# Bias tests on three engines and both bias sums on VectorE; the halves of a head's output added by GpSimd

## The chip, the cores and the metric

The kernel runs on one core of one Trainium2 chip. The core has five engines that run beside each other and meet at semaphores: TensorE (PE in the profile: matmuls, with PEld for its weight loads), VectorE (DVE), ScalarE (ACT), GpSimd (POOL) and SyncE (SP, which here only issues DMAs). The metric is the device time of one execution in microseconds, median of the runs. Each engine works through its own instructions in the order in which they stand in the program; an instruction that waits holds up all that stand behind it on that engine.

## The reference, cut to what matters

```python
scale = 1 / sqrt(64);  B, H, S, D = 2, 8, 576, 64;  hidden = 32
x = log1p(|i - j|) / log1p(max(i, 1))                      # i, j = 0..575
bias[h, i, j] = sum_d w2[d, h] * relu(x * w1[d] + b1[d])   # one for both batches
attn = softmax(scale * q @ k.T + bias)                     # float32
y = attn @ v                                               # (2, 8, 576, 64)
# then two feed-forward stages of matmuls over the 1152 rows of y ("moe" and "moe2")
```

The change lies in the first two stages alone: the bias, and the attention.

## The kernel before

**Order.** Nothing is moved by a scheduler: the instructions stand on each engine as the Python loops write them. Buffers come from pools of a fixed number of tiles, and whoever writes a tile again waits until its last readers are done.

**Bias.** relu(x*w1+b1) of a hidden unit changes slope at a knot, so the bias is a sum over tests "is |i-j| above the threshold of row i". One test tile `s` (128 partitions = 4 rows i by 32 hidden units, 576 columns j) is written per group g by `gen_s(g)`; there are 144 (`NG4`). `on_act` sends 3 of 8 to ScalarE as a steep sigmoid with bias `nthr` (L305), the others to VectorE as a comparison with `thr` (L307). `bias_mm(g16)` (L333) multiplies four test tiles by small weights `wb` into two PSUM tiles, `ps[0]` and `ps[1]`; there are 36 such steps (`NG16`). `bias_ev` (L343, L345) takes ScalarE to scale `ps[0]` into `t` and GpSimd to multiply `t` by a table `l16` (VectorE for the last two, `LASTV`); `bias_out` (L350) lets VectorE scale `ps[1]`, add `t` and write `bo`, which goes to DRAM. In step g16 the tests of step g16+2 are written. `sp` holds 12 test tiles. Ahead of the loop VectorE works out the knots (`one`, `eu`, `thr`, `nthr`; L236 to L265) and the weights (`big`, `sc`, `ab`, `wf`, `wb`; L269 to L296), one after the other, and the first eight tests stand among them. `prep_head(0, ...)`, GpSimd's high and low parts of q, k and v of head 0, is strewn over the odd steps.

**Attention.** 72 units u, nine per head (k = u mod 9), in a software pipeline with a step s per unit. In step s: TensorE's scores of unit s (`u_qk`, tile `sc`), its transposes of unit s-3 (`pt`, `pl`); VectorE's sum of scores and bias with row maximum of unit s-1 (`u_max`, tile `ng`, L430); ScalarE's exponential of unit s-2 (`u_exp`, L441) and high part of the transposed unit s-4 (`pth`, L505); VectorE's low part (`ptl`, L506). A head's product with v, `pv`, is made a head later in three chunks and ended at `EV`: k = 3 (512 columns), 6 and 8 (320 each). `pv` has its even part in one half of the partitions, its odd part in the other; `pv_ev` lets ScalarE copy one half across to `pvt` (L554) and VectorE add the other from PSUM (L556) into `x32`. `pvt` has two buffers. GpSimd makes the parts of the next head (`prep_head`, L66 and L195; v at k = 6 and 8) and, every second head, `x_out` (L568 to L570): six instructions in steps with k = 2 and 4 that multiply `x32` by 1/sum (`r`, brought by DMA) and split it for the next stage. `r` has one buffer, and SP brings it through DRAM (`r_d`), in line with the bias loads.

Of the kernel before, what the change touches and what calls it, by code (L numbers as in the profile page):

```python
# [55 lines left out]
def make_body(stop=None):  # L56
    def body(tc, a):
# [21 lines left out]
        with ctx, tc.manual_schedule():  # L79
# [128 lines left out]
            with ExitStack() as bctx:  # L208
# [37 lines left out]
                ts(sg, w1r, 0.0, ALU.is_ge, 2.0, ALU.mult)  # L246
                ts(sg, sg, -1.0, ALU.add)
                ts(dn, w1r, sg, ALU.mult, 1e-30, ALU.max)
                V.reciprocal(out=dn, in_=dn)
                ts(kap, b1r, sg, ALU.mult, dn, ALU.mult)  # L250

                ts(v, c4, kap, ALU.mult, -8.0, ALU.max)
                ts(v, v, 8.0, ALU.min, -1.4426950408889634, ALU.mult)
                ts(kf, v, MAGIC, ALU.add)
                ts(kf, kf, -MAGIC, ALU.add)
                V.tensor_tensor(out=f, in0=v, in1=kf, op=ALU.subtract)
                ts(pw.bitcast(I32), kf, 127.0, ALU.add, 2.0 ** 23, ALU.mult)
                taylor = [np.log(2.0) ** n / math.factorial(n) for n in range(8)]
                ts(po, f, float(taylor[7]), ALU.mult)
                for n in range(6, 0, -1):  # L260
                    V.scalar_tensor_tensor(out=po, in0=po, scalar=float(taylor[n]), in1=f, op0=ALU.add, op1=ALU.mult)
                V.scalar_tensor_tensor(out=po, in0=po, scalar=1.0, in1=pw, op0=ALU.add, op1=ALU.mult)
                ts(thr, po, sg, ALU.mult, sg, ALU.subtract)
                ts(rs, rr, sg, ALU.mult)

# [3 lines left out]
                V.tensor_reduce(out=m2, in_=w2a.rearrange("p (d h) -> p d h", h=H), op=ALU.max, axis=AX.X,  # L269
                                apply_absolute_value=True)  # L270
                V.tensor_reduce(out=m1, in_=wb1.rearrange("p (d t) -> p d t", t=2), op=ALU.max, axis=AX.X,
                                apply_absolute_value=True)
                V.tensor_tensor(out=m1, in0=m1, in1=m2, op=ALU.mult)
                V.tensor_reduce(out=top, in_=m1, op=ALU.max, axis=AX.X)
                V.tensor_scalar(out=top, in0=top, scalar1=2.0 ** -90, scalar2=None, op0=ALU.max)
                V.tensor_scalar(out=sc.bitcast(I32)[:, 0:1], in0=top.bitcast(I32), scalar1=0x7F800000, scalar2=0x7F800000,
                                op0=ALU.bitwise_and, op1=ALU.bitwise_xor)
                V.tensor_scalar(out=sc.bitcast(I32)[:, 1:2], in0=top.bitcast(I32), scalar1=0x7F800000, scalar2=None,
                                op0=ALU.bitwise_and)
                V.tensor_scalar(out=sc[:, 0:1], in0=sc[:, 0:1], scalar1=512.0, scalar2=None, op0=ALU.mult)  # L280
# [821 lines left out]
```

## Time and profile before

| | us |
|---|---|
| median of 3 runs (1149.09 to 1151.95) | 1149.34 |
| the profiled execution | 1150.27 |
| its span | 1148.5 |
| PE busy over the span | 1115.9 (97%) |
| DVE, ACT, POOL busy over the span | 711.9, 506.7, 373.3 |
| bias, from the first test to the last sum | 13.4 to 83.0 |
| attention, to the last exponential | 83 to 214 |

The profiled execution lies 0.93 us above the median, and 1.8 us of it lie around the span. Over the whole span TensorE is the busy engine; in the first 214 us VectorE is, with ScalarE and GpSimd close by, and the change lies there. A row of the timeline has start, length, engine, line, operation, output and input, and the count of merged instructions; in square brackets the idle time ahead of it and what ended that.

### The profile page before, as it was taken

The page shows a single profiled execution, that of the slowest core. Times are in us where ns is not written, and L with a number is a line of the kernel's source. Part 1 is how long each engine was busy: PE and PEld are TensorE (multiplying, and loading weights), DVE is VectorE, ACT ScalarE, POOL GpSimd, SP SyncE. Part 2 cuts the span into 40 slices and gives each one's busy share as a digit, 9 for nine tenths or more (in the row PEclk, how much of TensorE's full clock was granted, in tenths as well). Part 3 has the DMA queues.
Part 4 walks back from the last instruction along what each step waited for, and adds up shares of the span by engine and source line. Part 5 has one row for each costly group of instructions (what it writes and reads, how often), then busy time and mean ns, then how long its engine had stood idle before and what let it go on. Part 6 is the DMA issues. An engine that isn't in the chain of part 4 may idle for free.

```text
span 1148.5 us, 18982 instructions
## 1 busy us (share of the span) xinstructions
PE 1115.9 (97%) x7578; PEld 999.8 (87%) x7578; DVE 711.9 (62%) x1241; ACT 506.7 (44%) x879; POOL 373.3 (33%) x307
## 2 busy tenths in 40 slices
PE   6989999999999999999999999999999999999998
PEld 3448889999999899898998989989899898998986
DVE  7999999787752766554645636446365463554633
ACT  5988988633333553341522505325143151341520
POOL 3996789222212613220311202113022131220310
PEclk8999999999999999999999999999999999999999
DMA  3666665123310210210201102112021120210102
GB/s 140 229 230 216 210 187 166 41 92 110 111 42 14 93 37 13 62 47 28 74 26 49 49 27 74 37 38 70 14 65 40 34 74 10 64 47 28 56 19 82
DMA packets 35286, 87.45 MB, mean 76 GB/s; under 512 B 5439, under 2 KB 5630, under 8 KB 34302
## 3 DMA queue, kind: packets, MB, share of 16 engines
q1 hardware_dynamic: 35054, 85.96, 23.5%
q8 instruction: 59, 0.97, 0.3%
q10 hardware_dynamic: 144, 0.29, 0.1%
q14 instruction: 29, 0.24, 0.1%
HBM read 73.23 MB, written 13.01 MB: 75 GB/s over the span
## 4 chain that ended last, share of the span: by engine, by line
PE 70%; DVE 16%; issue 4%; ACT 2%; DMA 1%; DVEq 0%; ACTq 0%; SPq 0%
PE d L1014 34%; PE x L932 11%; PE y L932 8%; PE z L932 8%; PE o L810 3%; DVE ng L430 3%; DVE ptl L506 3%; PE m L584 2%; DVE ww L105 1%; DVE ww L108 1%; DVE ww L110 1%; DVE pth L506 1%; DVE x L556 1%; DMA wf<-in_moe_w 1%; ACT ww L104 1%
## 5 line engine op out<-in xcount | busy, mean ns | idle before, releaser
L1025 DVE SCALAR_TENSOR_TENSOR acc<-d,P,acc 128x512 f32<-128x512 f32 x135 | 101.3, 750 | 240.1 <-PE d L1014 240.0
L1000 POOL TENSOR_TENSOR w2l<-w2r,w2h 128x512 fp32r<-128x512 f32 x64 | 94.0, 1470 | 465.3 <-ACT w2h L999 457.0
L1014 PE MATMUL d<-w2h,hh 128*128 128x512 f32 x576 | 225.0, 391 | 0.0
L1014 PE MATMUL d<-w2h,hl 128*128 128x512 f32 x576 | 224.7, 390 | 0.0
L1014 PE MATMUL d<-w2l,hh 128*128 128x512 f32 x576 | 224.3, 389 | 0.0
L940 ACT ACTIVATE s<-x 128x576 f32<-128x576 f32 x96 | 62.5, 651 | 355.3 <-PE x L932 352.1
L945 ACT ACTIVATE hh<-s 128x576 fp32r<-128x576 f32 x128 | 87.9, 687 | 95.6 <-DVE s L957 46.3
L1014 PEld LDWEIGHTS d<-w2h,hl 128*128 128x128 f32 x576 | 108.1, 188 | 23.1 <-DVE hl L950 0.3
L1014 PEld LDWEIGHTS d<-w2l,hh 128*128 128x128 f32 x576 | 108.2, 188 | 22.1
L1014 PEld LDWEIGHTS d<-w2h,hh 128*128 128x128 f32 x576 | 108.2, 188 | 21.8
L950 DVE SCALAR_TENSOR_TENSOR hl<-s,hh 128x576 fp32r<-128x576 f32 x128 | 103.4, 826 | 1.7 <-ACT hh L945 1.5
L750 POOL TENSOR_TENSOR w1l<-wf,w1h 128x768 fp32r<-128x768 f32 x32 | 59.3, 1853 | 76.6 <-ACT w1h L749 76.6
L932 PE MATMUL x<-xth,w1h 128*128 128x288 f32 x384 | 82.6, 297 | 0.5 <-ACT acc L813 0.5
L932 PE MATMUL x<-xtl,w1h 128*128 128x288 f32 x384 | 82.2, 296 | 0.0
L932 PE MATMUL x<-xth,w1l 128*128 128x288 f32 x384 | 82.1, 295 | 0.0
L584 PE MATMUL m<-xh,wh 128*128 128x384 f32 x216 | 74.1, 343 | 1.8 <-DVE t L702 1.8
L333 PE MATMUL p<-s,wb 128*32 128x192 f16 (+1 forms) x1152 | 60.9, 295 | 13.1 <-DVE s L307 8.0
L584 PE MATMUL m<-xl,wh 128*128 128x384 f32 x216 | 73.6, 341 | 0.0
L584 PE MATMUL m<-xh,wl 128*128 128x384 f32 x216 | 73.5, 340 | 0.0
L333 PEld LDWEIGHTS <-wb 128*32 128x32 f16 x1152 | 31.8, 97 | 42.4 <-issue 31.1
L966 DVE TENSOR_TENSOR s<-y,s 128x576 f32<-128x576 f32 x32 | 24.2, 758 | 70.8 <-ACT w1h L753 58.9
L932 PEld LDWEIGHTS x<-xth,w1h 128*128 128x128 f32 x384 | 62.5, 188 | 2.0 <-ACT acc L813 0.7
(186 smaller groups left out, 2547.1 us busy)
## 6 DMA issues: line engine op xcount, KB each, us to landing
wf<-in_moe_w SPq DMA_DIRECT2D x32, 512.0 KB, 3.5
w2r<-in_moe_w SPq DMA_DIRECT2D x64, 256.0 KB, 2.6
bias_d<-bo SPq DMA_DIRECT2D x36, 288.0 KB, 2.7
bias<-bias_d SPq DMA_DIRECT2D x32, 288.0 KB, 3.6
wr<-in_moe_w SPq DMA_DIRECT2D x18, 512.0 KB, 3.7
qk<-in_qk SPq DMA_DIRECT2D x7, 1152.0 KB, 6.9
wr<-in_moe_w_out SPq DMA_DIRECT2D x6, 512.0 KB, 3.6
vr<-in_v SPq DMA_DIRECT2D x8, 320.0 KB, 4.3
```

The costliest lines, as they stand in the source:

```text
L333: T.matmul(out=thirds(pt)[32 * c:32 * c + 32, sl, :], lhsT=wb[p][:, q, :], rhs=s_t[4 * g16 + c][:, sl, :], start=(p == 0), stop=(p == 1))
L430: V.tensor_tensor_reduce(out=ng.rearrange("p (f n) -> p f n", f=2), in0=w["sc"][:, :, :SH], in1=bias_t[h, k // 2].rearrange("p (f n) -> p ...
L506: return lambda: V.tensor_tensor(out=lo, in0=src, in1=raw(hi), op=ALU.subtract)
L584: T.matmul(out=p[:, :TG], lhsT=ws[:, 128 * c:128 * c + 128], rhs=xs[:, c, TG * g:TG * g + TG], start=(c == 0 and n == 0), stop=(c == 3 and ...
L750: G.tensor_tensor(out=lo[:, 0:3], in0=t[:, 1:4], in1=raw(hi[:, 0:3]), op=ALU.subtract)
L932: T.matmul(out=ps[bank][:, s, :SH], lhsT=ws[:, i, c, :], rhs=xs[:, j, c, s * SH:s * SH + SH], start=(start and k == 0), stop=(k == 5), **kw)
L940: A.activation(out=t, in_=src, func=AF.Copy)
L945: A.activation(out=o, in_=src, func=AF.Relu)
L950: V.scalar_tensor_tensor(out=l, in0=src, scalar=0.0, in1=raw(o), op0=ALU.max, op1=ALU.subtract)
L1000: G.tensor_tensor(out=lo, in0=r, in1=raw(hi), op=ALU.subtract)
L1014: T.matmul(out=pd, lhsT=hs[:, fh, 128 * t:128 * t + 128], rhs=ws, start=(k == 0), stop=(k == 11))
L1025: V.scalar_tensor_tensor(out=acc[:, t, :], in0=pd, scalar=P[:, t, e:e + 1], in1=acc[:, t, :], op0=ALU.mult, op1=ALU.add)
```

## The change

- **Tests.** `TESTS`, a string of 24 letters, takes the place of `on_act`: of 24 tests 15 go to ScalarE, 4 to VectorE and 5 to GpSimd, which made none.
- **Sums.** `bias_ev` is one VectorE instruction: `ps[0]` times `ics` times the table. ScalarE's scaling and GpSimd's multiplication are gone, `LASTV` is not used any more. VectorE makes both sums of a step.
- **Head of the bias.** The instructions for the knots and for the weights stand alternately, and no test stands among them; `nthr` is made ahead of the first tests. Six pieces of `prep_head(0, ...)` are moved ahead of the loop, behind GpSimd's first two tests.
- **Attention, heads 0 to 6.** ScalarE copies both halves of `pv` to `pvt`; a DMA on SP's queue brings the other half across partitions into a new tile `pv2` (one buffer); GpSimd adds the two, two steps after the copy at the earliest (`adds`). Head 7 keeps the old way. The copies of the high part of v for heads 1 to 7 go from GpSimd to ScalarE. `ng` has two buffers instead of three.

```diff
+TESTS = "GAAVGAAAGAAVGAAVGAAAAAAV"
-def on_act(g):
-    return g > 3 and g % 8 in (2, 5, 7)
...
-                if part in (None, 0):
+                if part is None and k > 6:
+                    A.activation(out=hi, in_=src, func=AF.Copy)
+                elif part in (None, 0):
                     pool_copy(hi, src)
...
+                    kind = TESTS[g % len(TESTS)]
+                    if kind == "A":
+                        A.activation(out=s, in_=win, func=AF.Sigmoid, bias=nthr[:, g:g + 1], scale=STEEP)
                     else:
+                        eng = G if kind == "G" else V
+                        eng.tensor_scalar(out=s, in0=win, scalar1=thr[:, g:g + 1], scalar2=None, op0=ALU.is_gt)
...
+                for n in range(6):
+                    prep_head(0, (0, 2, 4, 6, 7, 8)[n // 3], n % 3)
...
-                    A.activation(out=v3(t), in_=thirds(ps[0]), func=AF.Copy, scale=ics[:, g16:g16 + 1])
-                    eng = G if g16 < NG16 - LASTV else V
-                    eng.tensor_tensor(out=t, in0=t, in1=l16[:, L16_OFF - 16 * g16:L16_OFF - 16 * g16 + S], op=ALU.mult)
+                    V.scalar_tensor_tensor(out=v3(t), in0=thirds(ps[0]), scalar=ics[:, g16:g16 + 1],
+                                           in1=v3(l16[:, L16_OFF - 16 * g16:L16_OFF - 16 * g16 + S]),
+                                           op0=ALU.mult, op1=ALU.mult)
...
-                    if g16 % 2:
+                    if g16 % 2 and g16 > 11:
...
-                    ng = up.tile([128, S], F32, tag="ng", name="ng", bufs=3)
+                    ng = up.tile([128, S], F32, tag="ng", name="ng", bufs=2)
...
-                    A.activation(out=tmp[om:om + 64, :n], in_=ps[oc:oc + 64, :n], func=AF.Copy)
+                    if h < H - 1:
+
+                        t2 = up.tile([128, 512], F32, tag="pv2", name="pv2", bufs=1)
+                        A.activation(out=tmp[:, :n], in_=ps[:, :n], func=AF.Copy)
+                        dma(t2[om:om + 64, :n], tmp[oc:oc + 64, :n])
+                        adds.append((9 * h + PV_AT[ch, bs] + 2, lambda: G.tensor_tensor(
+                            out=out, in0=v3(tmp[om:om + 64, :n]), in1=v3(t2[om:om + 64, :n]), op=ALU.add)))
+                    else:
+                        A.activation(out=tmp[om:om + 64, :n], in_=ps[oc:oc + 64, :n], func=AF.Copy)
+                        V.tensor_tensor(out=out, in0=v3(ps[om:om + 64, :n]), in1=v3(tmp[om:om + 64, :n]), op=ALU.add)
...
+                    while adds and adds[0][0] <= s:
+                        adds.pop(0)[1]()
```

What stands in a row on VectorE in the bias, before (`s` are tests, `bo` the sums):

```order
L307 TENSOR_SCALAR s<-rs,thr 128x3x192 x3
L350 SCALAR_TENSOR_TENSOR bo<-p,sc,t 128x576
L307 TENSOR_SCALAR s<-rs,thr 128x3x192 x2
L350 SCALAR_TENSOR_TENSOR bo<-p,sc,t 128x576
L307 TENSOR_SCALAR s<-rs,thr 128x3x192 x3
```

and after:

```order
L353 SCALAR_TENSOR_TENSOR t<-p,ics,tab_113 128x576
L360 SCALAR_TENSOR_TENSOR bo<-p,sc,t 128x576
L353 SCALAR_TENSOR_TENSOR t<-p,ics,tab_113 128x576
L323 TENSOR_SCALAR s<-rs,thr 128x3x192
L360 SCALAR_TENSOR_TENSOR bo<-p,sc,t 128x576
L353 SCALAR_TENSOR_TENSOR t<-p,ics,tab_113 128x576
L323 TENSOR_SCALAR s<-rs,thr 128x3x192
L360 SCALAR_TENSOR_TENSOR bo<-p,sc,t 128x576
```

Two sums and five tests per two steps have become four sums and, in two steps of three, one test between them.

GpSimd in head 3 of the attention (parts of k for head 4, `x_out` of heads 0 and 1, parts of v), before:

```order
L195 TENSOR_TENSOR kl_84<-qk,kh_80 128x576
L568 TENSOR_TENSOR x_2259<-x_2259,r 128x576
L66 TENSOR_SCALAR xh<-x_2259 128x576
L570 TENSOR_TENSOR xl<-x_2259,xh 128x576
L66 TENSOR_SCALAR kh_81<-qk 128x576
L195 TENSOR_TENSOR kl_85<-qk,kh_81 128x576
L568 TENSOR_TENSOR x_2259<-x_2259,r 128x576
L66 TENSOR_SCALAR xh<-x_2259 128x576
L570 TENSOR_TENSOR xl<-x_2259,xh 128x576
L66 TENSOR_SCALAR vs_88<-vr 128x5x64
L195 TENSOR_TENSOR vs_88<-vr,vs_88 128x5x64
```

and after:

```order
L194 TENSOR_TENSOR kl_84<-qk,kh_80 128x576
L587 TENSOR_TENSOR x_2223<-x_2223,r 128x576
L63 TENSOR_SCALAR xh<-x_2223 128x576
L589 TENSOR_TENSOR xl<-x_2223,xh 128x576
L63 TENSOR_SCALAR kh_81<-qk 128x576
L194 TENSOR_TENSOR kl_85<-qk,kh_81 128x576
L587 TENSOR_TENSOR x_2223<-x_2223,r 128x576
L63 TENSOR_SCALAR xh<-x_2223 128x576
L589 TENSOR_TENSOR xl<-x_2223,xh 128x576
L572 TENSOR_TENSOR x_2746<-pvt,pv_2748 64x2x256
L194 TENSOR_TENSOR vs_88<-vr,vs_88 128x5x64
L194 TENSOR_TENSOR vs_89<-vr,vs_89 128x5x64
```

The add of head 2's first chunk (L572, the 512 columns of k = 3) stands behind both halves of `x_out`, and the copies of v's high part are gone from this engine.

ScalarE in head 3 around the two later chunks (k = 6 and 8), with the semaphores that each waits for, before:

```order
L554 ACTIVATE pvt<-pv 64x320 [waits PE_49]
L505 ACTIVATE pth_1981<-pt 128x4x128 [waits PE_49]
L441 ACTIVATE pe,st<-ng,st 128x576 [waits DVE_49,Activation_49]
L505 ACTIVATE pth_1981<-pl 64x512 [waits PE_49]
L505 ACTIVATE pth_1982<-pt 128x4x128 [waits PE_49]
L441 ACTIVATE pe,st<-ng,st 128x576 [waits DVE_49,Activation_49]
L554 ACTIVATE pvt<-pv 64x320 [waits PE_49,Activation_49]
```

and after:

```order
L570 ACTIVATE pvt<-pv 128x320 [waits DMAHW1_49,Pool_49]
L515 ACTIVATE pth_1945<-pt 128x4x128 [waits PE_49]
L451 ACTIVATE pe,st<-ng,st 128x576 [waits DVE_49]
L515 ACTIVATE pth_1945<-pl 64x512 [waits PE_49]
L515 ACTIVATE pth_1946<-pt 128x4x128 [waits PE_49]
L451 ACTIVATE pe,st<-ng,st 128x576 [waits DVE_49]
L188 ACTIVATE vs_89<-vr 128x5x64 [waits PE_49]
L570 ACTIVATE pvt<-pv 128x320 [waits DMAHW0_49,Pool_49]
```

Each copy now waits for GpSimd: the copy at k = 8 takes the `pvt` buffer of the chunk at k = 3 of the same head, and its wait is for that chunk's add.

## Rows read from the trace of the kernel before

**Rows 1.** Busy us: stretch, length, PE, PEld, DVE, ACT, POOL; clock, DMA share, GB/s

```profile
13.20:83.00 69.80, 62.20 (x1160) 32.87 (x1160) 67.94 (x135) 62.39 (x91) 62.91 (x56) 0.96 0.58 200
83.00:214.00 131.00, 124.78 (x927) 115.79 (x927) 127.11 (x278) 115.68 (x266) 102.32 (x103) 0.99 0.57 180
```

**Rows 2.** Timeline, VectorE in the middle of the bias

```profile
61.31 1.35 DVE L307 TENSOR_SCALAR s<-rs,thr 128x576 f16<-128x576 f16 x3
62.57 0.81 DVE L350 SCALAR_TENSOR_TENSOR bo<-p,sc,t 128x576 f32<-128x576 f32 x1
63.30 0.93 DVE L307 TENSOR_SCALAR s<-rs,thr 128x576 f16<-128x576 f16 x2
```

**Rows 3.** Timeline, ScalarE in the middle of the bias

```profile
62.13 1.43 ACT L305 ACTIVATE s<-rs,nthr 128x576 f16<-128x576 f16 x2
```

**Rows 4.** Timeline, VectorE at the start and at the end of the bias

```profile
10.48 0.41 DVE L269 TENSOR_REDUCE big<-par 128x32 f32<-128x256 f32 x1
...
13.36 1.77 DVE L307 TENSOR_SCALAR s<-rs,thr 128x576 f16<-128x576 f16 x4
...
15.58 0.29 DVE L236 TENSOR_SCALAR nthr<-eu,one 128x144 f32<-128x144 f32 x1
...
19.51 0.82 DVE L350 SCALAR_TENSOR_TENSOR bo<-p,sc,t 128x576 f32<-128x576 f32 x1 [1.39 <-POOL t L345]
...
82.89 0.75 DVE L430 CUSTOM_DVE_ANT_0 ng<-sc,bias 128x576 f32<-128x576 f32 x1
```

**Rows 5.** GpSimd by line and shape, 13 to 83 us: count, busy, mean ns, idle before

```profile
L195 POOL TENSOR_TENSOR qs<-qk,qs 64x288 fp32r<-64x288 f32 x4 | 3.2, 799 | 0.3
L66 POOL TENSOR_SCALAR qs<-qk 128x576 fp32r<-128x576 f32 x4 | 3.1, 766 | 0.1
```

**Rows 6.** Instructions by line and shape, 83 to 214 us

```profile
L556 DVE TENSOR_TENSOR x<-pv,pvt 64x320 f32<-64x320 f32 x14 | 6.8, 482 | 0.2
L556 DVE TENSOR_TENSOR x<-pv,pvt 64x512 f32<-64x512 f32 x7 | 4.8, 682 | 0.1
...
L554 ACT ACTIVATE pvt<-pv 64x320 f32<-64x320 f32 x14 | 6.1, 433 | 0.3
...
L195 POOL TENSOR_TENSOR vs<-vr,vs 128x320 fp32r<-128x320 f32 x14 | 12.6, 897 | 1.2
...
L113 POOL TENSOR_TENSOR wl<-ww,wh 128x512 fp32r<-128x512 f32 x2 | 2.6, 1291 | 0.1
```

**Rows 7.** Timeline, GpSimd in heads 2 to 6

```profile
126.85 0.46 POOL L66 TENSOR_SCALAR vs<-vr 128x320 fp32r<-128x320 f32 x1 [2.05 <-PE pv L543]
...
128.23 0.68 POOL L66 TENSOR_SCALAR qs<-qk 128x576 fp32r<-128x576 f32 x1
...
145.63 0.46 POOL L66 TENSOR_SCALAR vs<-vr 128x320 fp32r<-128x320 f32 x1
...
161.56 0.46 POOL L66 TENSOR_SCALAR vs<-vr 128x320 fp32r<-128x320 f32 x1 [2.26 <-PE pv L543]
...
194.90 0.46 POOL L66 TENSOR_SCALAR vs<-vr 128x320 fp32r<-128x320 f32 x1 [0.43 <-PE pv L543]
```

**Rows 8.** Timeline, ScalarE's copy of head 2's last chunk

```profile
143.98 0.43 ACT L554 ACTIVATE pvt<-pv 64x320 f32<-64x320 f32 x1
```

**Rows 9.** Busy time, one head from last chunk to last chunk

```profile
195.45:211.42 15.97, 15.83 (x125) 15.19 (x124) 15.69 (x36) 14.56 (x34) 9.26 (x8) 1.00 0.39 122
```

**Rows 10.** Timeline, SP's queue in head 2

```profile
125.97 1.26 SPq L63 DMA_DIRECT2D r<-r_d  x2
```

**Rows 11.** DMA issues (count, KB each, us to landing)

```profile
bias<-bias_d SPq DMA_DIRECT2D x16, 144.0 KB, 3.0
out<-acc SPq DMA_DIRECT2D x9, 256.0 KB, 2.0
```

**Rows 12.** Clock granted to TensorE right after its wait at 81.4 to 83.7

```profile
84.00:86.00 2.00, 2.00 (x10) 1.98 (x10) 1.09 (x4) 1.30 (x4) 1.83 (x3) 0.50 0.87 260
```

**Rows 13.** Timeline, TensorE at the start of the attention

```profile
83.70 0.61 PE L413 MATMUL sc<-kh,qs 128*128 128x288 f32 x1 [2.32 <-DVE st L430]
```

More of the change, by code (lines that the diff above doesn't have):

```diff
@@ L245, in body @@
                 rs = bc.tile([128, L4_W], F16, name="rs")
[L246 to L264, printed above, removed]
                 big = bc.tile([128, 2 * HID + 1], F32, name="big")
@@ L268, in body @@
                 sc = bc.tile([128, 2], F32, name="sc")
[L269 to L280, printed above, removed]
@@ L294, in body @@
                 wb = [bc.tile([128, 2, 32], F16, name=f"wb{p}") for p in range(2)]
-                V.tensor_copy(out=wb[0], in_=wf)
-                V.tensor_tensor(out=wb[1], in0=wf, in1=wb[0], op=ALU.subtract)
                 ics = bc.tile([128, NG16], F32, name="ics")
+                stt = V.scalar_tensor_tensor
+                taylor = [float(np.log(2.0) ** n / math.factorial(n)) for n in range(8)]
+                knots = [
+                    lambda: ts(sg, w1r, 0.0, ALU.is_ge, 2.0, ALU.mult),
+                    lambda: ts(sg, sg, -1.0, ALU.add),
+                    lambda: ts(dn, w1r, sg, ALU.mult, 1e-30, ALU.max),
+                    lambda: V.reciprocal(out=dn, in_=dn),
+                    lambda: ts(kap, b1r, sg, ALU.mult, dn, ALU.mult),
+                    lambda: ts(v, c4, kap, ALU.mult, -8.0, ALU.max),
+                    lambda: ts(v, v, 8.0, ALU.min, -1.4426950408889634, ALU.mult),
+                    lambda: ts(kf, v, MAGIC, ALU.add),
+                    lambda: ts(kf, kf, -MAGIC, ALU.add),
+                    lambda: V.tensor_tensor(out=f, in0=v, in1=kf, op=ALU.subtract),
+                    lambda: ts(po, f, taylor[7], ALU.mult)]
@@ new lines, in body @@
+                knots += [lambda n=n: stt(out=po, in0=po, scalar=taylor[n], in1=f, op0=ALU.add, op1=ALU.mult)
+                          for n in range(6, 0, -1)]
+                knots += [
+                    lambda: stt(out=po, in0=po, scalar=1.0, in1=pw, op0=ALU.add, op1=ALU.mult),
+                    lambda: ts(thr, po, sg, ALU.mult, sg, ALU.subtract),
+                    lambda: ts(po, po, -1.5, ALU.add, MAGIC, ALU.add),
+                    lambda: ts(po, po, -MAGIC, ALU.add, 0.5, ALU.add),
+                    lambda: ts(nthr, po, sg, ALU.mult, -STEEP, ALU.mult)]
@@ new lines, in body @@
+                weights += [lambda q=q: V.tensor_tensor(
+                    out=wf[:, q, :].rearrange("p (i h) -> p i h", h=H),
+                    in0=ab[:, q, :].unsqueeze(1).to_broadcast([128, 4, H]),
+                    in1=msk.rearrange("p (i h) -> p i h", h=H), op=ALU.mult) for q in range(2)]
+                weights += [
+                    lambda: V.tensor_copy(out=wb[0], in_=wf),
+                    lambda: V.tensor_tensor(out=wb[1], in0=wf, in1=wb[0], op=ALU.subtract),
+                    lambda: ts(ics, ic16, sc[:, 1:2], ALU.mult)]
@@ L298, in body @@
+                weights.insert(10, lambda: ts(pw.bitcast(I32), kf, 127.0, ALU.add, 2.0 ** 23, ALU.mult))
+                for n in range(max(len(knots), len(weights))):
+                    for steps in (knots, weights):
+                        if n < len(steps):
+                            steps[n]()
+                    if n == 4:
+                        ts(rs, rr, sg, ALU.mult)
                 s_t = {}
@@ L531, in body @@
                 pvs = {}
+                adds = []
                 def pv_mm(h, ch, bs, i0, i1):
@@ L601, in body @@
                 EV = {3: (12, 0, (0, 1)), 6: (15, 1, (0,)), 8: (17, 1, (1,))}
+                PV_AT = {e[1:]: e[0] for e in EV.values()}
                 PREP = {0: 0, 1: 2, 2: 4, 3: 6, 6: 7, 8: 8}
```

42 lines of the change are left out of this document (19 added, 23 removed).

## The prediction, made before the changed kernel ran

> **What bounds the kernel now.** I read the busy times by stretch first, then the timelines of the bias and of the attention engine by engine, then the groups by shape and the DMA issues. From 231 us on the instructions are the same in both kernels, so I take that part as a shift and cost the first 214 us. In the bias VectorE is busy 67.9 of 69.8 us, ScalarE and GpSimd 62 to 63; in the attention VectorE 127 of 131, TensorE 125, ScalarE 116, GpSimd 102 [rows 1]. The reader is to see two things. No engine has much to give, so work moved off one can make another late. And the share of GpSimd is a mean: in the head that holds `x_out` it works from 128.23 to past 145.63 without a pause [rows 7], while in others it waits for TensorE (2.05 and 2.26 us ahead of the v parts at 126.85 and 161.56).
>
> **Bias, the pace.** A VectorE sum takes 0.73 us from start to start (62.57 to 63.30), a test 0.42 (61.31 to 62.57, three of them) [rows 2]. Before, two steps are 2 sums and 5 tests: 1.46 + 2.10 = 3.56 us, 1.78 a step. After, three steps are 6 sums and 2 tests, 4.38 + 0.84; in the step without a test the second sum needs the first one just ahead of it and waits out its length, 0.81 instead of 0.73 and a little, say +0.13: 5.35, again 1.78 a step. ScalarE has 2.5 tests a step at 1.43/2 = 0.715 [rows 3], 1.79 at most, and less where the next one starts before the last one's end: level with VectorE, no gain and no loss. So the pace stays.
>
> **Bias, the start.** `nthr` ends at 15.87 before. Ahead of it in VectorE's row stand the weights, 10.48 to 13.36 = 2.9 us, and four tests from 13.36 on, 1.7 [rows 4]. After, the weights' short steps lie in the pauses of the knots' chain and the tests come later: 15.9 - 4.6 = 11.3. ScalarE's two tests of step 0 end at 12.7, its next three at 14.8. GpSimd's part is the later one: behind its first two tests stand six pieces of q for head 0, two of 0.77 and four of 0.80 us [rows 5] = 4.7, and only then the test that step 2 needs. No row has a test on GpSimd. The nearest is its one-input pass over 128x576, 0.67 to 0.77 [rows 5]; the dear end is a two-input pass, 1.29 [rows 6]; the cheap end is 0.46, its pass over 320 columns [rows 7]. With 0.7: threshold at 10.7 (two of `nthr`'s steps of 0.29 ahead of it), two tests to 12.1, pieces to 16.8, test to 17.5, TensorE and first sum 0.8 later, so step 2 starts on VectorE at 18.3. Steps 2 to 33 take 32 x 1.78, step 34 has no test (1.6): the last step starts at 76.9 and its two sums end 1.7 later, 78.6. The first row of the attention, 82.89 before [rows 4], follows at about 78.9. **Bias: -4.0 us**; three tests at the dear end cost 1.8, so -1.9 to -4.8.
>
> **Attention, what VectorE gives back.** 14 adds of 0.48 and 7 of 0.68 us [rows 6], 11.6 us over seven heads, go. But VectorE is not far ahead of the next: from one last chunk to the next, 15.97 us, TensorE is busy 15.83 at full clock [rows 9], against 17.0 a head on average over four heads (126.85 to 194.90, [rows 7]). ScalarE has 14.56 in that head and gets two copies of 0.43 [rows 6, 9], 15.4. So a head can't go below about 16, whatever VectorE gives. I take 16.3 for a head that nothing else disturbs: two heads ahead of the first `x_out`, **-1.3** (-0.5 to -2.5); the last head, which keeps its adds, **-0.5** (0 to -1).
>
> **Attention, what GpSimd gets.** Per head +1.29 (the 512-column add, like the 128x512 pass) and 2 x 0.87 to 0.90 (like 128x320) [rows 6], less two copies of about 0.5 that go to ScalarE: +2. In heads without `x_out` its waits cover that. In heads 3 and 5 they don't. The order there is: parts of q, [weights part], part of q, add, part of k, `x_out`, part of k, `x_out`, then the add of the k = 3 chunk; and ScalarE's copy of the k = 8 chunk waits for that add, since `pvt` has two buffers. Behind that copy stand the exponentials and the `pth` of all following units, and behind its PSUM tile the next head's `pv` on TensorE. Before, ScalarE's copy starts at 143.98 [rows 8], and GpSimd ends `x_out` at 145.63 [rows 7]: already 1.65 too late for an add behind it, without the new work.
>
> The sum for one turn, from the v part at k = 8 of one head (126.85, bound by TensorE) to the same two heads on (161.56):
> - to the end of the add of the k = 6 chunk, which now stands ahead of the next head's parts. Its data come by the new DMA, in SP's row behind the two transfers of `r`, 125.97 + 1.26 [rows 10], and one bias load: issue at about 128.0. Landing: a 256 KB store takes 2.0, a 144 KB bias load 3.0 [rows 11]; this one has 80 KB and no DRAM end, 2.2 is near the lower. 130.2 + 0.9 = 131.1, 4.2 after 126.85. I take 4.1 for both turns. Least: copy 0.5, v part 0.9, add 0.9 = 2.3 without any wait; most 5.4.
> - GpSimd's row as before, 128.23 to 145.63 = 17.4 [rows 7], and two adds, 0.87 + 1.29: 19.6.
> - ScalarE from the freed copy over nine steps to the next v part: its own work, 15.4 to 15.5; with some waits 15.9 (15.5 to 16.6).
> 4.1 + 19.6 + 15.9 = 39.6 against 34.7: **+4.9**. The second turn (161.56 to 194.90 = 33.3 before) has no weights part, 1.3 less: 38.3, **+5.0**. Ends: +2.7 and +2.8; +6.9 each. The other heads' adds and the third DMA kind on SP's row I cost at nothing: GpSimd's waits of 2 us and the bias loads' lead of four tiles hide them; if SP stands behind GpSimd for `pv2`'s one buffer longer than that lead, VectorE waits for the bias and each turn costs some us more, which the upper end covers. Two buffers of `ng` cost nothing as long as ScalarE is less than a step behind.
>
> **Sum.** -4.0 - 1.3 + 4.9 + 5.0 - 0.5 = +4.1 on the profiled execution's 1150.27: 1154.4. That execution stood 0.9 over the median of 1149.34, so medians should show 1153.5 to 1154.4; I say 1154. All lower ends together: -2.8, all upper ones +11.4.
>
> The landing of the new DMA is the term without a row. The Trainium skill (DMA: Bandwidth & Descriptors, Anatomy of one DMA) gives 2.0 us fixed and bytes over 436 GB/s, for the software path: an estimate of 2.2 us for 80 KB, and the sum would stay. No run here shows a copy from SBUF to SBUF.
>
> **Rivals.**
> (1) GpSimd keeps up, and the engines take VectorE's gain. Then the two turns are four heads of 16.2, 64.8 instead of 68.05, -3.2, and all: -4.0 - 1.3 - 3.2 - 0.5 = -9, 1141. For it: GpSimd is busy only 102 of 131 us [rows 1]. Against it: the order on GpSimd, and 145.63 against 143.98. It decides if the copy at k = 8 finds its buffer free.
> (2) The stalls come, at their lower ends: the copies land early and ScalarE catches up. Two turns +5.5, with the early heads at their better end -2.5: -4.0 - 2.5 + 5.5 - 0.5 = -1.5, 1149.
> (3) TensorE loses its clock in each stall. At 83.70 it had waited 2.32 us [rows 13], and the next 2 us ran at 0.50, its lower level, 1.2 GHz [rows 12]. A stall of some 4 us in each turn could cost some 1.5 us more behind it: +3, 1157. Against it: TensorE has a lead to regain there and ScalarE is the slower one, so half of it may be hidden. The Trainium skill (TensorE: Matmul & The Clock Gate, HAM oscillation) says that matmuls start cold again after such idle gaps; the trace agrees with the 0.50 behind 2.32 us, and by it this would be the likely case.
> (4) Tests on GpSimd are dear, at the two-input price or above, and late all along: with two us of wait at the start and one in every sixth step behind, the bias gains nothing, +4.1 + 4.0 = +8, 1158. For it: nothing in the trace has this operation there. Against it: 5 tests in six steps (10.7 us) leave room even at 1.29.
>
> **How the numbers follow.** Forecast 0.47 (1151.5 to 1157), (1) 0.16, (2) 0.21, (3) 0.11, (4) 0.05. The range goes from 1147 to 1159: it holds the forecast, (2) for the most part, (3) and (4), and leaves out (1) and a little at either side. About 0.3%, 3.4 us, is what a measurement of this kernel can tell from no change: faster is under 1145.9, slower over 1152.8. Faster: (1) and a little of (2), 0.18. Slower: two thirds or more of the forecast (0.36), (3) and (4), 0.51. Same: the rest, 0.31.
>
> **What the changed profile would show.** VectorE's steps in the bias 1.78 us apart, first sum near 14 (the first `bo` was at 19.51, [rows 4]), the first `ng` near 79; if it is 81 or later, GpSimd's tests are dear. In the attention a wait of ScalarE at its copy (L570) for GpSimd, twice, of some 3 to 6 us, in heads 3 and 5, and TensorE and VectorE idle right behind it; the v parts at k = 8 some 39 us apart over two heads. VectorE no longer the one that never waits. Wrong would be a chain without GpSimd in the attention, or heads of 16 us throughout: then the buffer was free in time, and the price of GpSimd's row is mis-sized.

## The result, and the profile after

The changed kernel takes **1162.27 us** (median of four runs, 1161.3 to 1162.94), beside 1149.68 for the kernel before: a ratio of 1.0107, 95% interval 1.0094 to 1.012. It is slower by 12.6 us where I had forecast 4.1. It lies outside the range of 1147 to 1159, and 12.6 is more than all upper ends of my terms together (+11.4). The profiled execution has a span of 1161.1 us (before 1148.5), so the profiles show the same 12.6.

Busy time by stretch, in the columns of [rows 1]:

```profile
13.20:83.00 69.80, 57.91 (x1158) 31.22 (x1157) 63.66 (x96) 61.85 (x91) 66.45 (x53) 0.94 0.58 200
83.00:214.00 131.00, 116.06 (x846) 110.40 (x846) 107.33 (x235) 105.11 (x253) 97.97 (x96) 0.94 0.60 187
```

Every engine works less in the same 131 us of the attention than before (TensorE 116 instead of 125, GpSimd 98 instead of 102), although GpSimd was given work. So they wait for each other. GpSimd's timeline at the start of the bias, and VectorE's (start, length, line, operation; in brackets the idle time ahead and what ended it):

```profile
10.81 3.46 POOL L323 TENSOR_SCALAR s<-rs,thr 128x576 f16<-128x576 f16 x2 [9.15 <-DVE thr L235]
...
19.05 5.12 POOL L323 TENSOR_SCALAR s<-rs,thr 128x576 f16<-128x576 f16 x3
```

```profile
11.70 0.29 DVE L235 TENSOR_SCALAR nthr<-eu,one 128x144 f32<-128x144 f32 x1
...
14.70 0.82 DVE L353 SCALAR_TENSOR_TENSOR t<-p,ics,tab 128x576 f32<-128x576 f32 x1 [2.29 <-PE p L343]
...
21.55 0.82 DVE L353 SCALAR_TENSOR_TENSOR t<-p,ics,tab 128x576 f32<-128x576 f32 x1 [2.91 <-PE p L343]
...
50.77 0.81 DVE L353 SCALAR_TENSOR_TENSOR t<-p,ics,tab 128x576 f32<-128x576 f32 x1
...
56.15 0.81 DVE L353 SCALAR_TENSOR_TENSOR t<-p,ics,tab 128x576 f32<-128x576 f32 x1
...
82.85 0.76 DVE L440 CUSTOM_DVE_ANT_0 ng<-sc,bias 128x576 f32<-128x576 f32 x1
```

The threshold comes early (11.99 instead of 15.87), and three steps take 5.38 us (50.77 to 56.15), as summed. But a test on GpSimd takes 1.71 us (5.12 for three), and step 2 starts at 21.55 instead of the 18.3 that I had summed. The first attention row stands at 82.85, before at 82.89 [rows 4]: the bias gained nothing.

In the attention, who waited for whom (total us, times, longest), and ScalarE's copies that waited:

```profile
ACT pvt L570 <- POOL x L572: 19.0, 4, 6.8
...
PE pv L554 <- ACT pvt L570: 14.4, 4, 5.8
```

```profile
129.25 0.44 ACT L570 ACTIVATE pvt<-pv 128x320 f32<-128x320 f32 x1 [2.73 <-POOL x L572]
...
152.34 0.44 ACT L570 ACTIVATE pvt<-pv 128x320 f32<-128x320 f32 x1 [6.84 <-POOL x L572]
...
192.00 0.44 ACT L570 ACTIVATE pvt<-pv 128x320 f32<-128x320 f32 x1 [6.29 <-POOL x L572]
...
225.63 0.44 ACT L570 ACTIVATE pvt<-pv 128x320 f32<-128x320 f32 x1 [3.16 <-POOL x L572]
```

These are the copies of the last chunk of heads 1, 2, 4 and 6. The second and third are the two that I had forecast. What the waits did to the clockwork shows best in one row that every unit has, VectorE's `ng`: its start in the kernel before, and how much later (+) or earlier it stands in the others. "h3 k0" is the first unit of head 3; the last row is the end of the attention, the start of the last `xl`. The columns e2 to e10 belong to the experiments below.

| unit | before | after | e2 | e4 | e5 | e10 |
|---|---|---|---|---|---|---|
| h0 k0 | 82.89 | -0.04 | -0.09 | +0.22 | +0.15 | +0.56 |
| h2 k8 | 129.19 | -2.24 | -1.79 | -1.79 | -2.04 | -0.15 |
| h3 k0 | 130.48 | +0.48 | +0.28 | -1.77 | -2.05 | -0.15 |
| h4 k0 | 147.53 | +6.71 | +6.01 | +4.91 | -3.41 | -0.68 |
| h4 k8 | 163.90 | +5.89 | +5.17 | +2.96 | -0.34 | -1.31 |
| h5 k8 | 180.64 | +5.50 | +5.20 | +1.50 | -0.75 | -2.76 |
| h6 k0 | 181.91 | +11.80 | +11.50 | +9.12 | -0.42 | -2.46 |
| h6 k8 | 197.24 | +10.85 | +11.53 | +9.15 | +5.08 | -1.88 |
| h7 k8 | 212.71 | +10.56 | +11.31 | +9.12 | +4.86 | -1.22 |
| last `xl` | 231.07 | +13.72 | +12.12 | +9.12 | +4.30 | -1.77 |

The column "after" is a staircase: 2.24 us won over the first heads, then steps of +2.7, +6.0, +6.3 and, in the tail, +3.2, each about as long as the wait of ScalarE that belongs to it, and small gains in between. From the last `xl` on all kernels need the same to within 3 us (915.4 to 918.2 in the profiles).

### The profile page after: what moved, and what is told of

Read it like the earlier page. It is cut to its first block, busy times and chain, and to the rows that moved or that the text cites. A ratio compares the mean times of both kernels' runs of the same rounds, so it can differ in the third digit from the quotient of the medians.

```text
span 1161.1 us, 19036 instructions
## 1 busy us (share of the span) xinstructions
PE 1114.4 (96%) x7578; PEld 1002.9 (86%) x7578; DVE 698.2 (60%) x1187; ACT 507.5 (44%) x894; POOL 388.3 (33%) x310
## 4 chain that ended last, share of the span: by engine, by line
PE 72%; DVE 8%; POOL 5%; issue 3%; ACT 3%; DMA 2%; SPq 0%; POOLq 0%; DVEq 0%; ACTq 0%
PE d L1036 34%; PE x L954 12%; PE y L954 8%; PE z L954 8%; PE o L832 3%; PE m L603 2%; DMA pv<-pvt 2%; PE sc L423 1%; PE pv L554 1%; DVE ww L102 1%; POOL x L572 1%; DVE ww L107 1%; DVE ww L105 1%; PE pt L502 1%; POOL x L587 1%
## 5 line engine op out<-in xcount | busy, mean ns | idle before, releaser
L343 PE MATMUL p<-s,wb 128*32 128x192 f16 (+1 forms) x1152 | 57.5, 304 | 17.2 <-POOL s L323 10.2
L320 ACT ACTIVATE s<-rs,nthr 128x576 f16<-128x576 f16 x90 | 61.2, 762 | 12.0 <-DVE nthr L235 8.0
```

Source lines behind the costliest of these rows:

```text
L320: A.activation(out=s, in_=win, func=AF.Sigmoid, bias=nthr[:, g:g + 1], scale=STEEP)
L343: T.matmul(out=thirds(pt)[32 * c:32 * c + 32, sl, :], lhsT=wb[p][:, q, :], rhs=s_t[4 * g16 + c][:, sl, :], start=(p == 0), stop=(p == 1))
```

## The experiments

All ratios are to the kernel before, on the same chip, with 95% intervals.

**e1 and e2: each half alone.** e1 keeps the new bias and takes the attention of before; e2 the other way round.

> The bias of the changed kernel with the attention of the kernel before (VectorE adds, three ng buffers, GpSimd copies of v). Theory: the bias gains nothing because three tests on GpSimd at 1.70 us make its step 2 start 3.3 us later than I had summed, so the first attention row stands at about 82.9 and the whole time is that of before, 1149.7 (1148 to 1151). Rival: the new bias leaves head 0's parts on GpSimd later, and the attention pays for it in its first heads; then this kernel is some 2 to 4 us slower, 1152 to 1154, and part of the changed kernel's loss is the bias's.

> The bias of before with the attention of the changed kernel. Theory: the whole loss is made in the attention, by four waits of ScalarE for GpSimd's add (2.7, 6.8, 6.3 and 3.2 us in the changed kernel), so it takes 1162.3 (1160.5 to 1163.5) and shows the same four waits within 0.5 us each. Rival (the two parts disturb each other, for instance through where GpSimd stands at the first head): clearly under 1160, with fewer or shorter waits.

e1: 1146.67 us, 0.9976 (0.9964 to 0.9988). e2: 1160.81, 1.0097 (1.0074 to 1.012). So the loss is made in the attention alone: e2's column is the staircase again. Its four waits are 2.08, 6.86, 6.29 and 1.87 us; the first and the last are shorter by more than the 0.5 that I had allowed. In e1 I was wrong: the bias alone is some 3 us faster. Its first `ng` is only 0.22 early, as expected; the rest is won in head 0 (1.66 early behind it) and in the first units of head 1 (2.40). The windows there (columns of [rows 1]), e1 first, then the changed kernel:

```profile
84.00:86.00 2.00, 2.00 (x18) 1.89 (x17) 1.64 (x6) 1.53 (x5) 1.92 (x3) 1.00 0.74 207
```

```profile
84.00:86.00 2.00, 2.00 (x10) 1.98 (x10) 1.19 (x4) 1.33 (x4) 1.30 (x1) 0.50 0.85 244
```

At e1's start of the attention the granted clock stayed at 1.00 (2.4 GHz), while after and before [rows 12] it was 0.50 (1.2 GHz), and TensorE did 18 matmuls there instead of 10. By unit 5 of head 0, e1 is 1.67 us ahead of before and the changed kernel 0.30. The bias of the two is the same, and TensorE had waited 1.68 us in both just ahead; why the clock fell in one and not in the other, the rows don't show. The clock can be a part of e1's gain at most: in e3 (below), which has the same attention, it did fall (0.50 from 82 to 84 us), and from the first `ng` to unit 5 e3 still gained 1.05 us, e1 1.45 and the changed kernel 0.26.

**e8: the price of a test on GpSimd.** The changed kernel with these lines ahead of its first test (`gt` is a tile, `gx` and `gox` are fp32, `gh` and `goh` fp16):

```
+ G.tensor_scalar(goh, gh, gt[:, 0:1], None, is_gt)
+ G.tensor_scalar(goh, gh, 0.5, None, is_gt)
+ G.tensor_scalar(gox, gx, gt[:, 0:1], None, is_gt)
+ G.tensor_scalar(goh, gh, 2.0, None, mult)
+ G.tensor_scalar(goh, gx, gt[:, 0:1], None, is_gt)
+ G.tensor_scalar(goh, gh, gt[:, 0:1], 1.0, is_gt, mult)
+ G.tensor_scalar(goh, gh, 2.0, 1.0, mult, mult)
+ G.tensor_scalar(gox, gx, 2.0, 1.0, mult, mult)
```

> The changed kernel with eight extra operations of 128x576 on GpSimd ahead of its first test, into scratch tiles. In order: fp16 to fp16, greater-than with a threshold from a tile; the same with a constant; fp32 to fp32, greater-than with a tile's threshold; fp16 to fp16, times a constant; fp32 to fp16, greater-than; fp16 to fp16, greater-than and times one; fp16 to fp16, times two constants; fp32 to fp32, times two constants (the form of the copies that take 0.67 us). If the type is dear (fp16), the first, second, fourth, sixth and seventh take 1.7 and the third 0.7. If the compare is dear, those with greater-than take 1.7 and the products 0.7. If a single operation is dear where two in one instruction are not, the sixth to eighth take 0.7 and the others 1.7. The whole time says nothing here.

GpSimd's timeline, in the order of the lines (the one run took 1167.15 us):

```profile
2.73 1.73 POOL L234 TENSOR_SCALAR goh<-gh,gt 128x576 f16<-128x576 f16 x1 [1.07 <-DVE gt L233]
4.54 1.65 POOL L235 TENSOR_SCALAR goh<-gh 128x576 f16<-128x576 f16 x1
6.16 1.77 POOL L236 TENSOR_SCALAR gox<-gx,gt 128x576 f32<-128x576 f32 x1
7.91 1.66 POOL L237 TENSOR_SCALAR goh<-gh 128x576 f16<-128x576 f16 x1
9.66 1.86 POOL L238 TENSOR_SCALAR goh<-gx,gt 128x576 f16<-128x576 f32 x1
11.61 2.30 POOL L239 TENSOR_SCALAR goh<-gh,gt 128x576 f16<-128x576 f16 x1
14.00 0.68 POOL L240 TENSOR_SCALAR goh<-gh 128x576 f16<-128x576 f16 x1
14.64 0.67 POOL L241 TENSOR_SCALAR gox<-gx 128x576 f32<-128x576 f32 x1
```

None of my three cases fits as it stands. Type and threshold's place matter little; a compare costs 1.65 to 1.86, a single product (1.66) just as much, a compare with a product 2.30. Only the double product, the form of this kernel's copies, takes 0.67. Meeting VectorE isn't the reason: that engine stood idle from 2.62 to 4.95, all through the first compare. The row on which I had rested the price of a test, a copy [rows 5], was the one cheap form of those tried.

**e3 and e9: the start of the bias.** Both are e1 with other engines for the first twelve tests (G, A, V for GpSimd, ScalarE, VectorE); one of ScalarE's tests goes to VectorE as well:

```
  changed kernel:  GAAV GAAA GAAV
  e3:              VAAV VAAV VAAV
  e9:              GAAV VAAV VAAV
```

> The bias of the changed kernel with the first twelve tests on VectorE, ScalarE, ScalarE, VectorE and none on GpSimd, which starts with step 3; attention of before. Theory (the start is GpSimd's dear tests): first sum near 14, no wait of VectorE for step 2, step 3 at about 20.9 instead of 23.7, and from there 1.79 a step: first attention row at about 80, the whole 1146.9 (1146 to 1148). Rival (the start is ready early but the pace, or GpSimd's pieces of head 0, give it back): first row at 82 or later and 1149 to 1150.

> The bias of the changed kernel with one test on GpSimd in steps 0 to 2 (the first one of step 0) and VectorE's in place of the other two; attention of before. In the run without any such test there GpSimd's pieces of head 0 started at 8.8 us, and VectorE's short steps beside them took longer (a cast of 128x64 that takes 0.22 alone took 0.78), so the threshold came 2.8 us later. Here the one test waits for the threshold and keeps the pieces behind it. Theory (VectorE's short steps are slowed by GpSimd beside them): nthr ends at 12.0 again, first sum at about 13.5, step 3 at about 19.9 instead of 23.7, first attention row at about 79, the whole 1144.5 (1143 to 1147). Rival (the slow short steps were due to something else, or the pace gives the gain back): nthr after 14 or first row after 81, 1146.5 or more.

e3: 1147.83, 0.9979 (0.9969 to 0.9988). The time is in the theory's reach, but its mechanism fell: the first attention row stands at 82.94. With no test ahead of them, GpSimd's pieces of q started at 8.8 us, beside VectorE's chain of small steps. Two of those steps in e3, then the same two in the changed kernel, where GpSimd is idle:

```profile
10.57 0.78 DVE L300 CAST wb<-wf 128x64 f16<-128x64 f32 x1
...
12.99 0.89 DVE L235 TENSOR_SCALAR thr<-eu,one 128x144 f32<-128x144 f32 x1
```

```profile
9.51 0.18 DVE L300 CAST wb<-wf 128x64 f16<-128x64 f32 x1
...
10.36 0.35 DVE L235 TENSOR_SCALAR thr<-eu,one 128x144 f32<-128x144 f32 x1
```

The cast takes four times, the threshold two and a half times as long, and `nthr` ends at 14.75 instead of 11.99. Both end with a GpSimd instruction beside them: the cast at 11.35 (GpSimd's from 10.34 to 11.30), the threshold at 13.88 (GpSimd's to 13.79). e9 tells this apart from other reasons, since its one test on GpSimd waits for the threshold and holds the pieces back:

```profile
11.65 0.29 DVE L235 TENSOR_SCALAR nthr<-eu,one 128x144 f32<-128x144 f32 x1
...
79.39 0.76 DVE L440 CUSTOM_DVE_ANT_0 ng<-sc,bias 128x576 f32<-128x576 f32 x1
```

`nthr` is back at 11.94, the attention starts 3.5 us early, and the gain stays (-4.00 at h7 k8): **1144.06 us, 0.995 (0.9935 to 0.9964)**, faster than both kernels. So GpSimd's dear tests at the start were what the bias's gain had been lost to. The Trainium skill (SBUF — State Buffer, Who interferes with whom) says that casts and `tensor_scalar` on VectorE can hold, or be kept waiting by, a port that it shares with GpSimd. The trace agrees with the waiting, 0.78 us instead of 0.18; that a port is the reason no run here shows.

**e6: order on GpSimd.** One number in the changed kernel: the add of the k = 3 chunk is issued one step earlier, ahead of the second `x_out`.

```
- adds.append((9 * h + PV_AT[ch, bs] + 2, ...
+ adds.append((9 * h + PV_AT[ch, bs] + 2 - (ch == 0), ...
```

> The changed kernel with one number changed: the add of the k = 3 chunk is issued one step earlier, so it stands ahead of the second x_out on GpSimd instead of behind it. Buffers as in the changed kernel. Theory (order on GpSimd): x_out's three passes, 3.6 us, no longer lie ahead of that add, and the two big waits of ScalarE shrink by about 3.5 us each, 1155.5 (1154 to 1158). Rival (the landing of the copy is late anyway, so the add waits for its data and now holds GpSimd): the waits shrink by under 1.5 us each, over 1159.

1161.39, 1.01 (1.0083 to 1.0116): the time is the rival's, its mechanism only in part. GpSimd's waits in this kernel, two of its adds, and the two copies that had waited 6.84 and 6.29 (its profiled execution took 1165.33, 3.9 over the median):

```profile
POOL x L572 <- DMA pv<-pvt: 28.8, 11, 4.8
```

```profile
133.94 0.87 POOL L572 TENSOR_TENSOR x<-pvt,pv 64x320 f32<-64x320 f32 x1 [3.58 <-DMA pv<-pvt]
...
149.41 1.25 POOL L572 TENSOR_TENSOR x<-pvt,pv 64x512 f32<-64x512 f32 x1
```

```profile
150.70 0.44 ACT L570 ACTIVATE pvt<-pv 128x320 f32<-128x320 f32 x1 [5.49 <-POOL x L572]
...
191.16 0.44 ACT L570 ACTIVATE pvt<-pv 128x320 f32<-128x320 f32 x1 [1.60 <-POOL x L572]
```

The moved add itself (149.41) finds its data. But in the changed kernel GpSimd waited 17.2 us, nine times, for this DMA, here 28.8; the add of the k = 6 chunk (133.94) waits 3.58 instead of 0.96, and `x_out` starts 2 us later behind it. So the first big wait shrinks by 1.35 us, as the rival has it. The second shrinks by 4.69, as the theory has it, but others come in its place, 4.38 at the last chunk of head 3 and 2.67 at the first of head 5: ScalarE's eleven waits are 20.9 us in all, the four of the changed kernel 19.0.

**e4, e5, e10: one buffer after the other.** e4 sends the copy of the other half straight into `x`, so `pv2` with its one buffer goes. e5 gives `pvt` a third buffer in that room. e10 issues the loads of `r` three steps later on SP.

```
e4: - t2 = up.tile([128, 512], F32, tag="pv2", name="pv2", bufs=1)
    - dma(t2[om:om + 64, :n], tmp[oc:oc + 64, :n])
    + dma(out, v3(tmp[oc:oc + 64, :n]))
    - ... in1=v3(t2[om:om + 64, :n]), op=ALU.add)))
    + ... in1=out, op=ALU.add)))
e5: e4, and
    + tmp = up.tile([128, 512], F32, tag="pvt", name="pvt", bufs=3)
e10: e5, and
          dma(r_d[h], rt[0:9])
    +
    + def r_load(h):
    +     if h == H - 1:
    +         return
          if h % 2 == 0:
    ...
    - R = {2: (11, r_add, r_inv), 3: (12, r_tr), 4: (13, r_out)}
    + R = {2: (11, r_add, r_inv), 3: (12, r_tr), 4: (13, r_out), 7: (16, r_load)}
```

> The changed kernel, but the copy between the two halves goes straight into x, where GpSimd then adds the other half in place; the buffer pv2, of which there was one, is gone, so SP no longer waits for GpSimd's last add before it issues the next copy. pvt keeps its two buffers. Theory (the two big waits of ScalarE, 6.8 and 6.3 us, come from GpSimd's order, the add of the k = 3 chunk behind x_out; only the two smaller ones, 2.7 and 3.2 us, come from the copy's late issue and landing): the small ones go or halve, the big ones stay within 1 us, 1157 (1155 to 1160). Rival (the one buffer of pv2 on SP's row is the cause of all four): all shrink, under 1153.

e4: 1158.52, 1.0073 (1.0058 to 1.0088), the theory: the two smaller waits are gone, the two larger ones stay. They are longer, 8.0 and 7.6 us (the second by 1.3, over the 1 us that I had allowed), since ScalarE now comes to them earlier, to the first at 142.6 instead of 145.5.

```profile
ACT pvt L569 <- POOL x L571: 15.6, 2, 8.0
```

> As the one before, and a third buffer of pvt in the room that pv2 left, so ScalarE's copy of the k = 8 chunk doesn't need the add of the k = 3 chunk. Theory (ScalarE's wait for that add is the loss): all four waits go, the gain of VectorE in the early heads (2.2 us in two) stays and repeats in the later ones, 1148 (1144 to 1151). Rival (GpSimd has too much work in the heads with x_out, wherever it is waited for): the wait moves to TensorE, which waits for GpSimd's v parts or q and k parts of the next head, and the time stays over 1154.

e5: 1153.7, 1.0036 (1.0024 to 1.0047), neither. ScalarE's wait for the add is gone (1.2 us in all), and at h4 k0 it is the earliest of the table (-3.41). But at h4 k2 and h6 k2 it falls back, and VectorE waits there for something new:

```profile
153.07 0.76 DVE L440 CUSTOM_DVE_ANT_0 ng<-sc,bias 128x576 f32<-128x576 f32 x1 [2.23 <-DMA bias<-bias_d]
...
190.04 0.76 DVE L440 CUSTOM_DVE_ANT_0 ng<-sc,bias 128x576 f32<-128x576 f32 x1 [2.33 <-DMA bias<-bias_d]
```

SP's queue and GpSimd's timeline ahead of the first:

```profile
135.65 0.56 SPq L60 DMA_DIRECT2D r_d<-rt  x1
147.60 1.31 SPq L60 DMA_DIRECT2D r<-r_d  x2
149.01 0.55 SPq L60 DMA_DIRECT2D bias<-bias_d  x1
```

```profile
146.16 1.42 POOL L586 TENSOR_TENSOR x<-x,r 128x576 f32<-128x576 f32 x1
```

SP stands from 136.2 to 147.6, until GpSimd's last `x_out` has read the one buffer of `r`, and the bias loads stand behind it.

> As the run with the direct copy and three pvt buffers (1153.7), and the two loads of r are issued three steps later (k = 7 instead of k = 4), behind the bias loads that they held back. In that run ScalarE no longer waited for GpSimd's add, but in heads 4 and 6 VectorE waited 2.2 and 2.3 us for a bias load, since SP stood at the load of r until GpSimd's last x_out had read r's one buffer. Theory (that wait on SP is what is left): the two waits for the bias go, and with them the TensorE waits right behind, 1148.5 (1147 to 1150.5). Rival (GpSimd's row itself is too long in these heads): VectorE or TensorE then waits for GpSimd's parts of k and q instead, 1152 or more.

e10: 1147.29, 0.9979 (0.997 to 0.9989), the theory: no wait of VectorE for the bias is left, and the staircase is flat. TensorE's waits for GpSimd's part of k, the rival, are still there, and small (1.2 us in two places).

**e11 to e13: the halves put together.** e11 is e10's attention with e9's bias. e12 adds on GpSimd only for heads whose adds fall between the heads with `x_out`. e13 also gives the copies of v back to GpSimd.

```
e12: - if h < H - 1:
     + if h in (0, 1, 3, 5):
e13: e12, and
     - if part is None and k > 6:
     + if part is None and k > 8:
```

> The attention of the run before (direct copy, three pvt buffers, late load of r) with the bias of the run that has one GpSimd test in steps 0 to 2. Theory: the two gains add, 5.8 us less than that attention run gives beside the bias of the changed kernel, which itself gained less behind this attention; 1143 (1140.5 to 1145.5). Rival (the early start of the attention is given back, since its first head is held by ScalarE's copies of v, as in the changed kernel): over 1146.

> As the run before, but only heads 0, 1, 3 and 5 have their halves added by GpSimd; their adds fall into heads without x_out, where GpSimd waits anyway. The adds of heads 2, 4 and 6, which fall into the heads with x_out, stay on VectorE. Theory (GpSimd is short only in the heads with x_out): those heads run as in the kernel before and the others gain about 1 us each, 1141 (1139 to 1143.5), faster than with all adds on GpSimd. Rival (with the waits on SP gone GpSimd keeps up everywhere): slower than the run before by 1 to 2 us.

> As the run with the adds of heads 0, 1, 3 and 5 on GpSimd (1142.0), with the copies of v's high parts back on GpSimd instead of ScalarE. All kernels that have these copies on ScalarE and GpSimd free beside them lose 1.15 us between head 0's last row and head 1's first; there one operation of VectorE (128x512, int32, with a constant) took 1.67 us instead of 0.44 beside GpSimd's parts of q. Theory (that loss is VectorE's operation meeting GpSimd's, not ScalarE's copies, 0.45 us each): where GpSimd stands in head 0 decides, ScalarE's copies cost little; the whole stays within 1 us of the run before, 1141 to 1143. Rival (ScalarE is the engine that sets the pace of a head, and 0.9 us a head come back): 1139 or less.

e11: 1143.41, 0.9948 (0.9933 to 0.9963). e12: **1142.03, 0.9932 (0.9918 to 0.9947)**. e13: 1142.01, 0.9927 (0.9911 to 0.9944). The ranges of e11 and e12 hold, but the two gains don't add as the theory of e11 had it: e11 is 3.9 us under e10, not 5.8, and level with e9 (0.995). With all adds on GpSimd the attention gains nothing clear over that of before, and with some of them (e12, whose four runs all lie under the four of e11) two us at best. e13 takes what e12 takes, as its theory has it, so ScalarE's copies don't cost the 3 us of the rival; its four runs lie between 1140.54 and 1144.87, too wide to tell a microsecond. The 1.15 us at the start of head 1 are gone in e13. The operation of VectorE there, in the changed kernel and in e13, and GpSimd beside it in the changed kernel:

```profile
96.00 1.67 DVE L103 TENSOR_SCALAR ww<-ww 128x512 int32<-128x512 int32 x1
```

```profile
92.58 0.52 DVE L103 TENSOR_SCALAR ww<-ww 128x512 int32<-128x512 int32 x1
```

```profile
95.97 1.42 POOL L194 TENSOR_TENSOR qs<-qk,qs 64x576 fp32r<-64x576 f32 x1
```

In its profile, which is the slowest of the four, e13 loses 2.5 us at the start of head 6 instead, where TensorE waits 1.08 us for GpSimd's part of k.

## Why the prediction was wrong, step by step

**Bias, the pace: right.** 5.38 us for three steps, summed 5.35.

**Bias, the start: wrong by 4.0, a mis-sized term.** The test was taken at 0.7 us with a dear end of 1.29, both from other operations. It takes 1.71 (none of e8's compares is cheaper than 1.65), above both ends. By my own chain: two tests end at 14.24 instead of 12.1, pieces at 18.9, third test at 20.7, step 2 at 21.55 instead of 18.3; some 0.7 more until step 5 make up the rest. My rival (4) had the dear test and the lost start, though not the lateness all along, and its chance of 0.05 was far too low. e9 gives 3.5 of the summed 4.0 back once two of the three tests go elsewhere: the first row was forecast at 78.9 and stands at 79.39.

**Early heads: -2.24 for -1.3**, inside the bounds, in spite of 1.15 lost at the start of head 1.

**The two turns: the second right, the first short by 3.2.** From h2 k8 to h4 k8 the shift grows by 8.13 (summed 4.9), from there to h6 k8 by 4.96 (summed 5.0). The waits that I had forecast came, in size too: 6.84 and 6.29, with GpSimd's add behind `x_out`. e4 and e5 show that mechanism: with a free buffer they go. What the sum lacked is the smaller wait ahead, 2.73. Its step is the one costed at nothing, "the other heads' adds and the third DMA kind on SP's row". The add of head 1's k = 3 chunk, and SP's queue ahead of it:

```profile
127.95 1.26 POOL L572 TENSOR_TENSOR x<-pvt,pv 64x512 f32<-64x512 f32 x1 [2.38 <-DMA pv<-pvt]
```

```profile
121.27 0.48 SPq L60 DMA_DIRECT2D pv<-pvt  x1
121.80 0.51 SPq L60 DMA_DIRECT2D r_d<-rt  x1
126.71 1.26 SPq L60 DMA_DIRECT2D r<-r_d  x2
```

ScalarE had the copy ready at 118.0. SP issues it at 121.27, when GpSimd's add of the chunk before (120.38 to 121.24) has left `pv2`, and it lands 6.7 us later, beside the loads of q, k and v. The next copy, that of the k = 6 chunk, goes out at 129.24, when the add above has left `pv2`; I had summed 128.0. The three terms of the first turn, from v part to v part (now on ScalarE) over the ends of the two adds:

```profile
126.06 0.45 ACT L188 ACTIVATE vs<-vr 128x320 fp32r<-128x320 f32 x1
...
131.95 0.86 POOL L572 TENSOR_TENSOR x<-pvt,pv 64x320 f32<-64x320 f32 x1 [0.96 <-DMA pv<-pvt]
...
151.06 1.25 POOL L572 TENSOR_TENSOR x<-pvt,pv 64x512 f32<-64x512 f32 x1
...
168.62 0.47 ACT L188 ACTIVATE vs<-vr 128x320 fp32r<-128x320 f32 x1
```

They are 6.75, 19.50 and 16.31 us, where I had summed 4.1 (at most 5.4), 19.6 and 15.9: the way of the copy to its add is the term that failed. Those of the second turn, over 173.17 and 191.97 to 207.19, are 4.55, 18.80 and 15.22 for 4.1, 18.3 and 15.9, so the second is right to 0.7 us in each term, and not by luck.

The landing was mis-sized as well; DMA issues of the attention (count, KB each, median us):

```profile
pv<-pvt SPq DMA_DIRECT2D x14, 80.0 KB, 3.1
...
pv<-pvt SPq DMA_DIRECT2D x7, 128.0 KB, 5.3
```

I had 2.2 for the smaller ones, near the lower of my two rows. The formula of the Trainium skill (DMA: Bandwidth & Descriptors, Anatomy of one DMA) gave the same 2.2, as an estimate for the software path. The trace, with 3.1 on SP's queue and under this load, doesn't agree with it.

**The last head: +3.16 for -0.5.** Head 6's adds stand behind the last `x_out`, and the copy at 225.63 waits as the others do. I had counted two turns, up to the `x_out` that stands in head 5, and left out the third, in head 7.

The terms measured: 0 - 2.24 + 8.13 + 4.96 - 0.29 + 3.16 - 1.1 (from the last `xl` on) = 12.6.

**Rival (1)** needs the free buffer. e10 beside e1 (0.9979 and 0.9976) and e11 beside e9 (0.9948 and 0.995) show that even then the attention with all adds on GpSimd gains nothing clear over that of before. **Rival (3)**, the clock: it fell behind the stalls as it said, but cost nothing there that lasts. Behind the first wait (columns of [rows 1]):

```profile
128.00:131.00 3.00, 1.26 (x9) 1.27 (x10) 0.74 (x2) 1.75 (x5) 2.91 (x3) 0.94 0.79 215
131.00:134.00 3.00, 3.00 (x15) 2.95 (x15) 2.86 (x7) 2.66 (x7) 1.88 (x3) 0.50 0.44 115
```

TensorE runs three us at its lower level, yet the shift, which had grown by 2.72 at h3 k0 for a wait of 2.73, is the same three units later (+0.48 and +0.54). Behind the second, with the clock at 0.50 from 152 to 157 us, it is +6.71 at h4 k0 and stays between +6.26 and +7.18 over the next five units. At the start of the attention, where TensorE is the one waited for, e1 may have won some tenths by keeping its clock; that is one profile, set beside e3's 1.05 us without it, and not shown by an experiment of its own.

**What stays open.** e1 and e2 add up to 7.4 us, the changed kernel lost 12.6. In the profiles e1 stands at -1.51 at h7 k8 and at -2.12 at the last `xl`; with e2 that is 9.8, 0.8 under the changed kernel, and 10.0, 3.7 under it. e1's clock may be part of the 0.8. Of the 3.0 that come on in the last head, 1.3 is the last wait, 1.87 us in e2 and 3.16 in the changed kernel; the rest I can't place.

## What to carry to other kernels

When work moves to an engine that has no row for that very operation, the nearest row isn't a price: look at which form the row is (here a product of two constants, the only cheap one of those tried), or put the dear end well above it. When a step goes through a new buffer, write down for each single-buffered tile who frees it and what stands behind the waiter in an in-order queue: here `pvt`, `pv2` and `r` each hid the next one, and taking away one only showed the next. Give an idle engine work where it is idle (heads without `x_out`: e12, 1.4 us under e11), not on average.

## What the runs showed of the hardware that I had not expected

- One pass of GpSimd over 128x576: 0.67 us for a product with two constants, 1.65 to 1.86 for a compare or a single product, 2.30 for a compare and a product; the compare with a threshold in a tile and the double product, each tried in fp16 and in fp32, differ by 0.04 us at most (e8).
- Small VectorE operations beside a busy GpSimd: a cast of 128x64 0.78 instead of 0.18 (e3), an operation of 128x512 with a constant 1.67 instead of 0.52 (the changed kernel and e13). In e3 each slow one ends 0.04 to 0.09 us behind the end of a GpSimd instruction. The `scalar_tensor_tensor` steps of 128x144 between them kept their 0.3 us, but each starts within 0.03 us of such an end, so e3 doesn't show whether they would wait too.
- A copy of 80 KB between halves of the on-chip memory, issued by SP beside other loads, lands after 3.1 us, one of 128 KB after 5.3 (medians, the changed kernel).
